# A planned attention and maxout kernel: a new order for its head and first ten groups, key values in pairs of chunks, five relu slots

## The chip, the cores and the metric

The kernel runs on one core of a Trainium2 chip. The time is that of one execution on the device, in microseconds (us), taken as the median of several runs. [...] Matmul results lie in PSUM, which has eight banks of 128 partitions by 512 floats; everything else lies in SBUF.

## What is computed

Agent attention is followed by a maxout feed-forward layer. There are 4 batches of 12544 tokens with 128 channels, 49 agents per batch, and a hidden width of 768.

```python
def sm(a, b):
    s = scale * (a @ b.transpose(0, 2, 1))
    s = s - s.max(-1, keepdims=True)
    e = np.exp(s)
    return e / (e.sum(-1, keepdims=True) + 1e-09)
agent_v = sm(agents, k) @ v          # per batch 49 x 128
x = sm(q, agents) @ agent_v          # per token 128
h = np.maximum(np.maximum(x @ w1, x @ w2), x @ w3)
out = h @ w_out
```

## The kernel before

**The algebra.** The kernel never forms x. For each batch it multiplies `agent_v` with weight differences into one array `G` (49 rows, held in both halves of the partitions): `(w3-w1)`, `(w2-w1)`, and a linear part `w1 @ w_out`. The maximum of three is then w1's part plus a maximum of differences, so a query group needs two matmuls per 128 hidden columns, a relu of the first (op `a`, ACT) and a maximum of the second with it (op `x`, DVE). For one of the six column blocks (`FI` = 4) the differences are nested, and both steps are relus on ACT. The part with w1 goes straight to the output as a linear term (`li`).

**Stage one, per batch b:** the keys and values come in chunks of 9 x 128 tokens. For each chunk g: load (`kl`, `vl`), cast to bf16 (`kc`, `vc`), transpose the keys (`kt`, by PE in batch 0, by DMA later), scores against the agents (`ks`), exponential (`kx`, ACT), values times exponentials (`kv`, nine matmuls), and the addition of this product to a running sum (`va`, DVE). The exponentials are summed by POOL (`ea`, `fo`) in batches 1 to 3, by matmuls with ones (`to`) in batch 0. Then the sum is normalised (`nr`) and the products `gp` and their casts `gv` make `G`. In batch 0 this is the head: nothing of the queries' main work can start before `nr0`. Later batches run beside the queries.

**Stage two:** 49 query groups s of 1024 tokens: load `ql`, cast `qc` (POOL), transpose (`qt` and its copy `qe`, or by DMA, `qd`), scores `sc`, exponential `ex`, sums `su` and their reciprocal `re`; for each block f `u`, `a`, `v`, `x`; the output matmuls `p` into two PSUM banks with `li`, scaling `ov` (DVE), store `st`.

**The order.** `graph` (line 208) lists all operations with their engine, what they follow, and which tile slots they use. The order of all of them, with the slot numbers, is written out by hand of a planner in `ORDER` (line 826): each engine executes its operations in that order and waits with semaphores where an operation needs a result or a slot that is not free yet (`Plan.waits`). SP's loads stand in the same order, so a load that waits for a slot holds up the loads behind it. `SLOTS` (line 46) says how many slots each class has: 8 banks `PS`, 13 load tiles `LD`, 3 relu tiles `AS`, 4 tiles each `EK` for exponentials of keys and `VB` for cast values, 13 tiles `R` for maxima, 10 output tiles `OS`. `SPLIT` says which relus are done in halves (two instructions of 512 columns on two separate banks, "u"). `ROWS` says which output matmuls run as pairs on half the array's rows. `warm` matmuls (`wm`, `wn`) in the head work on nothing.

In batches 1 to 3 a chunk's scores, its value product and, for the last chunk, the total share one PSUM bank `m` from `ks` to `va`:

```python
add(f"kv{r}", PE, em.values(b, g, n, m), mm(n, 49), after=[f"kx{r}", f"vc{r}"], use=[m, f"vb{r}", f"e{r}"])
add(f"va{r}", DVE, em.add_values(b, g, m), (0.13, 0.25), after=[f"kv{r}"] + ([f"va{b}.{g - 1}"] if g else []),
    use=[m, plan.tile("VA", f"va{b}")])
```

Of the kernel before, what the change touches and what calls it, by code (L numbers as in the profile page):

```python
# [9 lines left out]
FP32 = mybir.dt.float32  # L10
BF16 = mybir.dt.bfloat16
# [16 lines left out]
rrfrff rrrffr ffrfff ffrfrr rfffff rrrrrr ffffff ffffrr fffrff rfrrfr fffffr ffrfrf rrfrrr fffffr fffffr frffrf fffrrr rfffff  # L28
# [26 lines left out]
class Plan:  # L55
# [152 lines left out]
def graph(plan, em):  # L208
# [6 lines left out]
    add("agl", ACT, em.load_agents, (0.5, 5.0), dma=True)  # L215
    add("agc", DVE, em.cast_agents, (0.42, 0.52), after=["agl"])
    add("agt", PE, em.turn_agents, (0.2, 0.4), after=["agc", "id"], new=[("PS", "agt")])
    add("prep", DVE, em.place_agents, (0.4, 0.5), after=["agt", "ones"], use=["agt"])
    ch = chunks(0)
    for g, (t0, n) in enumerate(ch):  # L220
# [4 lines left out]
        add(f"kt0.{g}", PE, em.k_turn(g, n), mm(n, 128), after=[f"kc0.{g}", "prep"], new=[("PS", f"kT_ps0.{g}", 3)], use=[f"kb0.{g}"])  # L225
# [3 lines left out]
            new=[("EK", f"e0.{g}")], use=[f"s0.{g}"])  # L229
        add(f"to0.{g}", PE, em.totals(g, n), mm(1, n * 49), after=[f"kx0.{g}"], use=[f"e0.{g}", plan.tile("PS", "acc")])  # L230
        m = n if n == KT else 2
        add(f"vc0.{g}", ACT, em.cast("v", "vb", 0, t0, n, ACT, 0, m), act(m * 128), after=[f"vl0.{g}"], new=[("VB", f"vb0.{g}")],
            use=[f"v0.{g}"])
        if m < n:
            add(f"vd0.{g}", DVE, em.cast("v", "vb", 0, t0, n, DVE, m, n), ((n - m) * 0.067 + 0.08, (n - m) * 0.067 + 0.2),
                after=[f"vl0.{g}"], use=[f"v0.{g}", f"vb0.{g}"])
        add(f"kv0.{g}", PE, em.first_values(g, n), mm(n, 49), after=[f"to0.{g}", f"vc0.{g}"] + ([f"vd0.{g}"] if m < n else []),
            use=[f"vb0.{g}", f"e0.{g}", "acc"])
    for g in range(SPARE):
        add(f"wm.{g}", PE, em.warm(f"warm.{g}"), (0.2225, 0.45), after=["id"], new=[("PS", f"warm.{g}")])  # L240
    for g in range(len(ch)):
        add(f"wn.{g}", PE, em.warm(f"warn.{g}", 2), (0.445, 0.67), after=["id", f"vl0.{g}"], new=[("PS", f"warn.{g}")])
    last = len(ch) - 1
    for w in ("w1", "w3", "w2"):
        add(f"l{w}a", SP, em.w_load(w, 0, DFF // 2), new=[("LD", w)], **dma(196))
        add(f"l{w}b", SP, em.w_load(w, DFF // 2, DFF), use=[w], **dma(196))
    add("lwo", SP, em.w_load("wo", 0, DFF), new=[("LD", "wo")], **dma(393))
    add("d31a", DVE, em.differences(C31, "w3", "w1", ((0, DFF // 2),)), (0.43, 0.55), after=["lw1a", "lw3a"], use=["w1", "w3"])
    add("d31b", DVE, em.differences(C31, "w3", "w1", ((DFF // 2, FI * P), (FI * P + P, DFF))), (0.42, 0.54), after=["lw1b", "lw3b"],
        use=["w1", "w3"])  # L250
    add("d32", DVE, em.differences(C31, "w3", "w2", ((FI * P, FI * P + P),)), (0.21, 0.33), after=["lw2b", "lw3b"], use=["w2", "w3"])
    add("d21a", DVE, em.differences(C21, "w2", "w1", ((0, DFF // 2),)), (0.43, 0.55), after=["lw2a", "lw1a"], use=["w1", "w2"])
    add("d21b", DVE, em.differences(C21, "w2", "w1", ((DFF // 2, DFF),)), (0.43, 0.55), after=["lw2b", "lw1b"], use=["w1", "w2"])
    add("cw1", ACT, em.cast_w1, (0.74, 0.87), after=["lw1a", "lw1b"], use=["w1"])
    add("tw1", PE, em.turn_w1, mm(NF, 128), after=["cw1", "prep"], new=[("PS", "tw1")])
    add("ew1", DVE, em.evacuate_w1, dve_half(DFF), after=["tw1"], use=["tw1"])
    add("cwo", POOL, em.cast_wo, (0.77, 0.85), after=["lwo"], use=["wo"])
    add("rs0", DVE, em.reduce_first, (0.5, 0.6), after=[f"to0.{g}" for g in range(last + 1)], new=[("KR", "kr0")], use=["acc"])
    add("rc0", DVE, em.recip_first, (0.35, 0.4), after=["rs0"], use=["kr0"])
    add("nr0", DVE, em.normalise_first, (0.13, 0.25), after=["rc0"] + [f"kv0.{g}" for g in range(last + 1)], new=[("G", "G0")],  # L260
        use=["kr0", "acc"])
    half = DFF // 2
# [50 lines left out]
    for s in range(NQ):  # L313
# [741 lines left out]
```

## Time and profile before

| | us |
|---|---|
| median of 3 runs | 439.33 (438.46 to 439.44) |
| span of the profiled execution, first to last instruction | 436.6 |
| last value cast of batch 0 on ACT, start | 38.47 |
| first relu of group 0 (ACT), start | 41.90 |
| first maximum of group 0 (DVE), start | 43.02 |
| mean time of a maximum over 1024 columns (DVE) | 1.219 |
| mean time of a relu over 1024 columns (ACT) | 1.033 |

The device time of the profiled execution itself is not listed; its span is 2.7 us below the median. In the profile's rows all operations have the line 388, that of the helper that records them, so rows are told apart by their tiles: `AS` is the first relu's output, `R` the maximum's, `OS` the scaled output, `KB`/`VB` cast keys and values, `EK` the exponentials of the keys, `VA` the running sum of values, `avT` the normalised values of the agents, `wall` the weight differences, `G` the product. "<-" in brackets names what ended the wait ahead of an instruction.

### The profile page before, as it was taken

Reading aid. Unit: us, or ns where it says so; the run is one execution under the profiler, and the core shown is the slowest. Engines: PE = TensorE matmul, PEld = TensorE weight load, DVE = VectorE, ACT = ScalarE, POOL = GpSimd, SP = SyncE. Lnnn points to the kernel's source line nnn. Section 1 sums busy time; section 2 is a strip of 40 time slices with the busy share of each in tenths; the row PEclk is TensorE's granted clock in tenths of the full one; section 3 lists DMA queues with packets and bytes.
Section 4 is the critical chain, followed back from the end, with each engine's and each line's share of the span. In section 5 each row is a group of like instructions: output and inputs, shape, how many; then the busy total and the mean of one; then the engine's idle time right before and its main releaser. Section 6 shows DMA issues by size and latency. Waiting matters only on the chain.

```text
span 436.6 us, 14853 instructions
## 1 busy us (share of the span) xinstructions
PE 411.9 (94%) x6488; PEld 256.9 (59%) x6488; DVE 386.6 (89%) x470; ACT 393.9 (90%) x486; POOL 170.0 (39%) x177
## 2 busy tenths in 40 slices
PE   1788999999999999999999999999999999999994
PEld 1464565666666566656656655656656555655574
DVE  1435999999999999999998999899999999999994
ACT  1278999999999999999999899999999999999993
POOL 3541565556655535165525445342531111000000
PEclk9989999999999999999999999999999999999999
DMA  8999999999999999999999999996999994266313
GB/s 310 411 410 383 311 334 372 289 281 343 269 318 342 279 371 298 266 339 285 294 345 261 407 247 278 276 326 143 276 363 290 284 306 98 74 208 208 119 71 125
DMA packets 98107, 122.37 MB, mean 280 GB/s; under 512 B 71479, under 2 KB 74235, under 8 KB 98043
## 3 DMA queue, kind: packets, MB, share of 16 engines
q1 hardware_dynamic: 97552, 121.07, 95.2%
q8 instruction: 51, 0.84, 0.8%
q10 hardware_dynamic: 491, 0.36, 0.3%
q14 instruction: 13, 0.11, 0.1%
HBM read 78.74 MB, written 25.69 MB: 239 GB/s over the span
## 4 chain that ended last, share of the span: by engine, by line
PE 69%; ACT 16%; DVE 7%; DMA 4%; issue 2%; POOL 1%; SPq 0%; POOLq 0%
PE ps L388 69%; ACT AS L388 9%; DVE R L388 6%; DMA LD<-in_k_dram 4%; ACT R L388 2%; ACT ps L388 2%; POOL KB L388 1%; DVE OS L388 1%; ACT EQ L388 1%; ACT VB L388 1%; ACT G L388 1%; ACT EK L388 1%; ACT OS L388 0%; SPq L388 0%; DVE QT L388 0%
## 5 line engine op out<-in xcount | busy, mean ns | idle before, releaser
L388 DVE TENSOR_TENSOR R<-ps,AS 128x1024 bf16<-128x1024 f32 x245 | 293.5, 1219 | 15.1 <-PE ps L388 10.7
L388 ACT ACTIVATE AS<-ps 128x1024 bf16<-128x1024 f32 (+1 forms) x259 | 245.8, 987 | 10.0 <-PE ps L388 7.2
L388 PE MATMUL ps<-EQ,G 49*128 49x512 bf16 (+1 forms) x1248 | 203.3, 370 | 3.5 <-ACT AS L388 0.7
L388 PE MATMUL ps<-wo_bf,R 64*128 64x128 bf16 (+1 forms) x3368 | 194.0, 218 | 1.1 <-issue 0.8
L388 PEld LDWEIGHTS ps<-wo_bf,R 64*128 64x128 bf16 (+1 forms) x3368 | 139.5, 95 | 59.4 <-issue 31.3
L388 PEld LDWEIGHTS ps<-EQ,G 49*128 49x128 bf16 x1248 | 56.4, 93 | 63.8 <-DVE R L388 18.3
L388 POOL CAST QB<-LD 128x1024 bf16<-128x1024 f32 x49 | 50.5, 1040 | 94.6 <-DMA QT<-QB 49.8
L388 POOL CAST KB<-LD 128x1152 bf16<-128x1152 f32 (+2 forms) x45 | 49.8, 1115 | 52.1 <-DMA LD<-in_k_dram 41.8
L388 DVE TENSOR_TENSOR OS<-ps,RC 128x512 f32<-128x512 f32 x96 | 65.4, 682 | 2.6 <-PE ps L388 2.2
L388 POOL CAST VB<-LD 128x1152 bf16<-128x1152 f32 (+1 forms) x33 | 37.4, 1136 | 40.7 <-DMA LD<-in_v_dram 36.5
L388 ACT ACTIVATE ps<-ps 128x1024 f32<-128x1024 f32 x49 | 49.9, 1018 | 2.8 <-PE ps L388 2.2
L388 ACT ACTIVATE R<-ps 128x1024 bf16<-128x1024 f32 x49 | 50.3, 1027 | 1.9 <-PE ps L388 1.6
L388 ACT ACTIVATE EK<-ps 128x441 bf16<-128x441 f32 (+2 forms) x45 | 23.4, 535 | 18.8 <-PE ps L388 18.4
L388 POOL TENSOR_TENSOR EA<-EA,EK 128x441 f32<-128x441 f32 x27 | 27.6, 1022 | 25.4 <-ACT EK L388 25.1
L388 ACT ACTIVATE EQ<-ps 128x512 bf16<-128x512 f32 x49 | 29.9, 610 | 1.0 <-PE ps L388 0.5
L388 DVE COPY KT<-ps 128x1152 bf16<-128x1152 bf16 (+1 forms) x12 | 8.2, 701 | 14.0 <-PE ps L388 14.0
L388 PE MATMUL ps<-QT,agT 128*64 128x512 bf16 (+1 forms) x104 | 19.9, 388 | 0.2
L388 PE MATMUL ps<-G,EQ 49*128 49x128 bf16 x392 | 19.1, 217 | 0.0
L388 PE MATMUL ps<-EK,VB 128*128 128x49 bf16 x392 | 17.4, 186 | 1.6 <-ACT VB L388 1.6
L388 PEld LDWEIGHTS ps<-EK,VB 128*128 128x128 bf16 x392 | 13.9, 97 | 8.1 <-ACT EK L388 4.2
L388 PE MATMUL ps<-agT,KT 128*128 128x49 bf16 x392 | 17.4, 186 | 0.4 <-DVE KT L388 0.4
L388 PEld LDWEIGHTS ps<-agT,KT 128*128 128x128 bf16 x392 | 14.4, 98 | 4.7 <-issue 2.1
(59 smaller groups left out, 177.6 us busy)
## 6 DMA issues: line engine op xcount, KB each, us to landing
LD<-in_q_dram SPq DMA_DIRECT2D x48, 512.0 KB, 7.7
out_dram<-OS SPq DMA_DIRECT2D x48, 512.0 KB, 6.2
LD<-in_k_dram SPq DMA_DIRECT2D x40, 576.0 KB, 7.6
LD<-in_v_dram SPq DMA_DIRECT2D x40, 576.0 KB, 8.4
LD<-in_k_dram SPq DMA_DIRECT2D x3, 512.0 KB, 5.3
LD<-in_v_dram SPq DMA_DIRECT2D x3, 512.0 KB, 6.7
LD<-in_moe_w_dram SPq DMA_DIRECT2D x6, 192.0 KB, 10.6
KT<-KB SPq DMA_TRANSPOSE x33, 7.3
```

Source lines behind the costliest of these rows:

```text
L388: i = call(*args, **named)
```

## The change

- The operations ahead of the first matmul of group 10 stand in a new order. From there on the order is the old one, apart from operations that no longer exist or were moved across that point (`ov.8.1`, two stores and a few loads), and with other slot numbers.
- Batch 0's keys and values come in 12 chunks of 8 and one of 2 instead of ten of 9 and two of 4. Keys are loaded first, most values behind them, into output tiles (`OS`) that are not in use yet. The casts of the values are spread over ACT, POOL and DVE (`VCAST`). The exponentials lie in `R` tiles. The totals get a PSUM bank of their own.
- Each of w1, w2 and w3 is loaded in three parts (columns 0 to 127, 128 to 383, 384 to 767), and the differences and batch 0's `G` are made in these parts. The cast of w1 moves from ACT to POOL.
- In batches 1 to 3 the value products of two chunks are added up in one PSUM bank of its own, and `va` runs once per pair: 6 times instead of 11 per batch.
- `AS` has five slots instead of three.
- In groups 0 to 9, 12 relus (2 before) and 21 maxima (none before) are done in halves.
- `G`'s linear part is kept in two column blocks, each filled in one half of the partitions only, the rest set to zero once by POOL (`gz`); the matmuls of `li` read their block. (A variant over the whole array, `out_linear_half`, exists and is not used: `LINEAR` is "b" everywhere.)
- The casts `gv` are given to engines by `OUTS`; in batches 1 and 2 one more of them is on DVE.
- `wn` issues three matmuls instead of two, for 13 chunks.

```diff
-FIRST = [KT] * 10 + [4, 4]
+AGAIN = (3,) * 13
+CUTS = {"a": (0, P), "b": (P, 3 * P), "c": (3 * P, DFF)}
+FIRST = [GT] * 12 + [2]
...
 SPLIT = """
-...... u..... .u.... ...... ...... ...... ...... ...... ...... ...... .u.u.. uu.... ...... ...... ...... ...u.. ..u... ......
+v.v..b vbvv.. v.u..v uv.... .....v uv.v.u ..v... .b.u.v v.vb.b .uuv.. .u.u.. uu.... ...... ...... ...... ...u.. ..u... ......
...
+LINEAR = "bbbbbbbbbbbbbbbbbbbbbbbbbbbbbbbbbbbbbbbbbbbbbbbbb"
+VCAST = "aapapapppaaad"
+CASTW = "p"
+OUTS = ("aaadadd", "addda", "addda", "adada")
...
-SLOTS = {"PS": 8, "LD": 13, "QB": 3, "KB": 3, "VB": 4, "KT": 4, "QT": 4, "EQ": 4, "EK": 4, "AS": 3,
+SLOTS = {"PS": 8, "LD": 13, "QB": 3, "KB": 3, "VB": 4, "KT": 4, "QT": 4, "EQ": 4, "EK": 4, "AS": 5,
...
+    add("gz", POOL, em.clear_linear, (0.6, 0.7), after=["id0"])
...
-        add(f"vl0.{g}", SP, em.kv_load("v", 0, t0, n), new=[("LD", f"v0.{g}")], **dma(n * 65.536))
+        add(f"vl0.{g}", SP, em.kv_load("v", 0, t0, n), new=[("OS" if g < 10 else "LD", f"v0.{g}")], **dma(n * 65.536))
...
-            add(f"kv{r}", PE, em.values(b, g, n, m), mm(n, 49), after=[f"kx{r}", f"vc{r}"], use=[m, f"vb{r}", f"e{r}"])
-            add(f"va{r}", DVE, em.add_values(b, g, m), (0.13, 0.25), after=[f"kv{r}"] + ([f"va{b}.{g - 1}"] if g else []),
-                use=[m, plan.tile("VA", f"va{b}")])
+            if g % 2 or g == len(ch) - 1:
+                two = [(x, ch[x][1]) for x in range(g // 2 * 2, g + 1)]
+                y, h = f"{b}.{g // 2}", f"y{b}.{g // 2}"
+                add(f"kv{y}", PE, em.values(b, two, h), mm(sum(x[1] for x in two), 49), after=[f"{z}{b}.{x}" for x, _ in two for z in ("kx", "vc")],
+                    new=[("PS", h)], use=[f"{z}{b}.{x}" for x, _ in two for z in ("vb", "e")])
+                add(f"va{y}", DVE, em.add_values(b, g // 2, h), (0.13, 0.25), after=[f"kv{y}"] + ([f"va{b}.{g // 2 - 1}"] if g > 1 else []),
+                    use=[h, plan.tile("VA", f"va{b}")])
...
+                if SPLIT[s][f] in "vb":
+                    vs = [f"{v}.{h}" for h in range(2)]
+                    add(v, PE, em.hidden(vs, s, f, C21, True), pe, mode=ROW, after=[f"ex.{s}"] + needs(1), new=[("PS", x) for x in vs],
+                        use=[e] + gs)
+                    for h in range(2):
+                        add(f"x.{s}.{f}.{h}", DVE, em.max_second(vs[h], s, f, h), (0.6, 0.72), after=[v, f"{a}.{h if SPLIT[s][f] == 'b' else 0}"],
+                            use=[vs[h], a, r])
...
+    def clear_linear(self):
+        for i in range(SLOTS["G"]):
+            self.nc.gpsimd.memset(self.slots["G", i][:, C1O:], 0.0)
...
     def product_out(self, b, c0, c1, base, name, eng):
         def fn():
             src, out = self.t[name][:, c0 - base:c1 - base], self.t[f"G{b}"][:, c0:c1]
-            if eng == ACT:
-                self.nc.scalar.activation(out, src, AF.Copy)
-            else:
-                self.nc.vector.tensor_copy(out=out, in_=src)
+            cuts = [(src, out)] if c0 < C1O else [(src[h * H:(h + 1) * H, :], self.t[f"G{b}"][h * H:(h + 1) * H, c0 + h * C:c1 + h * C]) for h in range(2)]
+            for src, out in cuts:
+                if eng == ACT:
+                    self.nc.scalar.activation(out, src, AF.Copy)
+                else:
+                    self.nc.vector.tensor_copy(out=out, in_=src)
...
 ORDER = """
...
+vc0.7/0 kv0.7 to0.10 kx0.3/10 vc0.5/2 wn.5/2 to0.3 vl0.4/6 wn.3/2 vc0.0/1 vc0.3/3 wn.0/5 wn.4/2 sc.0/4 kv0.3 vl0.8/7 vc0.8/0 wm.2/1 kv0.8
+to0.8 vl0.6/8 wn.6/1 to0.2 vl0.11/2 to0.0 rs0/0 wn.11/2 vl0.2/9 vc0.4/3 kv0.4 vc0.6/0 kv0.6 kv0.5 wn.8/2 kv0.0 gz rc0 lw2a/5 lw1a/7 d21a
+vc0.11/3 ex.0/0 kv0.11 lw1b lw3b/4 d31b vc0.2/0 kv0.2 nr0/0 gpb0/1 gvb0 lw3a d31a gpa0/4 gva0 gpd0/2 lw2b d21b gpe0/5 u.0.1/0,1 gve0
...
```

More of the change, by code (lines that the diff above doesn't have):

```diff
@@ L228, in graph @@
         add(f"kx0.{g}", ACT, em.k_exps(0, g, n, f"s0.{g}"), (n * 0.041 + 0.07, n * 0.041 + 0.2), after=[f"ks0.{g}"],
[L229 to L232, printed above, removed]
+            new=[("R" if g < 9 else "EK", f"e0.{g}")], use=[f"s0.{g}"])
@@ L233, in graph @@
+        add(f"to0.{g}", PE, em.totals(g, n), mm(1, n * 49), after=[f"kx0.{g}"], use=[f"e0.{g}", plan.tile("PS", "tot")])
+        eng = ENGINES[VCAST[g]]
+        add(f"vc0.{g}", eng, em.cast("v", "vb", 0, t0, n, eng, 0, n), act(n * 128), after=[f"vl0.{g}"], new=[("VB", f"vb0.{g}")],
             use=[f"v0.{g}"])
-        if m < n:
-            add(f"vd0.{g}", DVE, em.cast("v", "vb", 0, t0, n, DVE, m, n), ((n - m) * 0.067 + 0.08, (n - m) * 0.067 + 0.2),
-                after=[f"vl0.{g}"], use=[f"v0.{g}", f"vb0.{g}"])
@@ L247, in graph @@
     add("lwo", SP, em.w_load("wo", 0, DFF), new=[("LD", "wo")], **dma(393))
[L248 to L256, printed above, removed]
+    for x, (c0, c1) in CUTS.items():
+        cuts = ((c0, FI * P), (FI * P + P, c1)) if x == "c" else ((c0, c1),)
+        add(f"d31{x}", DVE, em.differences(C31, "w3", "w1", cuts), dve(c1 - c0), after=[f"lw1{x}", f"lw3{x}"], use=["w1", "w3"])
+        add(f"d21{x}", DVE, em.differences(C21, "w2", "w1", ((c0, c1),)), dve(c1 - c0), after=[f"lw1{x}", f"lw2{x}"], use=["w1", "w2"])
@@ new lines, in graph @@
+                add(f"a.{s}.{f}.0", ACT, em.relu(u, u, None), (0.917, 1.076), after=[u], use=[u])
+                add(v, PE, em.hidden([u], s, f, C21, False), pe, mode=ROW, after=[f"a.{s}.{f}.0"] + needs(1), use=[u, e] + gs)
+                if SPLIT[s][f] == "d":
+                    add(f"x.{s}.{f}.0", DVE, em.relu(r, u, None, DVE), (1.14, 1.28), after=[v], use=[u, r])
+                else:
+                    add(f"x.{s}.{f}.0", ACT, em.relu(r, u, None), (0.917, 1.076), after=[v], use=[u, r])
@@ L352, in graph @@
                 else:
-                    add(u, PE, em.hidden([u], s, f, C31, True), pe, mode=ROW, after=[f"ex.{s}"] + needs("a", "b"), new=[("PS", u, 3)], use=[e] + gs)
-                    add(a, ACT, em.relu(a, u, None), (0.917, 1.076), after=[u], use=[u, a])
-                add(v, PE, em.hidden([v], s, f, C21, True), pe, mode=ROW, after=[f"ex.{s}"] + needs("c", "d"), new=[("PS", v, 3)], use=[e] + gs)
-                add(f"x.{s}.{f}", DVE, em.max_second(v, s, f), (1.14, 1.28), after=[v] + ([f"{a}.{h}" for h in range(2)] if two else [a]),
-                    use=[v, a, r])
@@ L358, in graph @@
-        lin = ["gvl" if p[0] == 0 else f"gvl{p[0]}" for p in parts]
+                    add(u, PE, em.hidden([u], s, f, C31, True), pe, mode=ROW, after=[f"ex.{s}"] + needs(0), new=[("PS", u, 3)], use=[e] + gs)
+                    add(f"{a}.0", ACT, em.relu(a, u, None), (0.917, 1.076), after=[u], use=[u, a])
+                if SPLIT[s][f] in "vb":
[5 more added lines that the diff above has]
+                            use=[vs[h], a, r])
+                else:
+                    add(v, PE, em.hidden([v], s, f, C21, True), pe, mode=ROW, after=[f"ex.{s}"] + needs(1), new=[("PS", v, 3)], use=[e] + gs)
+                    add(f"x.{s}.{f}.0", DVE, em.max_second(v, s, f, None), (1.14, 1.28), after=[v] + [f"{a}.{h}" for h in range(1 + (SPLIT[s][f] == "u"))],
+                        use=[v, a, r])
```

600 lines of the change are left out of this document (317 added, 283 removed).

## The prediction

> **What bounds the kernel now.** I read the page's busy line and tenths first, then the windows, the waits, the groups by shape, and the timeline of the start.
>
> ```profile
> span 436.6 us, 14853 instructions
> PE 411.9 (94%) x6488; PEld 256.9 (59%) x6488; DVE 386.6 (89%) x470; ACT 393.9 (90%) x486; POOL 170.0 (39%) x177
> PE   1788999999999999999999999999999999999994
> DVE  1435999999999999999998999899999999999994
> ACT  1278999999999999999999899999999999999993
> PE 69%; ACT 16%; DVE 7%; DMA 4%; issue 2%; POOL 1%; SPq 0%; POOLq 0%
> ```
>
> A slice is 10.9 us. Three engines are full from the fifth slice to the last but one; only the first four have room. The chain of waits runs over PE for 69% of its length, but with ACT and DVE inside it: there is no single bound. The windows put numbers on both stages (columns: busy us of PE, PEld, DVE, ACT, POOL with counts, clock, DMA share, GB/s; the two rows with four columns show PE alone):
>
> ```profile
> 20.00:25.00 5.00, 4.12 (x60) 1.00 1.02 406
> 25.00:30.00 5.00, 3.81 (x62) 0.70 1.03 412
> 35.00:40.00 5.00, 4.18 (x58) 1.00 1.05 382
> 42.00:60.00 18.00, 16.79 (x254) 9.75 (x254) 17.23 (x22) 17.69 (x26) 10.45 (x10) 1.00 1.07 339
> 60.00:80.00 20.00, 19.85 (x320) 12.22 (x314) 18.93 (x23) 18.81 (x22) 13.62 (x15) 1.00 1.17 303
> 80.00:100.00 20.00, 19.91 (x346) 13.17 (x344) 19.56 (x24) 18.72 (x23) 10.37 (x10) 1.00 1.09 327
> 100.00:122.00 22.00, 22.00 (x332) 13.44 (x328) 21.12 (x28) 20.97 (x26) 15.45 (x16) 1.00 1.10 305
> 122.00:430.00 308.00, 304.56 (x4870) 188.24 (x4869) 294.00 (x341) 295.62 (x361) 105.85 (x110) 1.00 0.93 260
> ```
>
> Until 40 us the DMA engines are full at about 0.41 MB per us: the head is bound by its loads. From 42 us on, groups 0 to 9 take until 122. There DVE is busy 17.23+18.93+19.56+21.12 = 76.8 of 80 us and ACT 76.2: **3.2 and 3.8 us** of idle time is all that a better order of these groups can win. In 122 to 430 DVE idles 14.0 us, ACT 12.4, and PE is full by its modelled ends.
>
> **The change, part by part.**
>
> *The head.* First its end in the trace of before:
>
> ```profile
> 37.99 0.59 ACT L388 ACTIVATE EQ<-ps 128x512 bf16<-128x512 f32 x1
> 38.47 1.16 ACT L388 ACTIVATE VB<-LD 128x1152 bf16<-128x1152 f32 x1
> 39.12 0.56 DVE L388 TENSOR_TENSOR wall<-LD,LD 128x384 bf16<-128x384 f32 x1 [0.70 <-DMA LD<-in_moe_w_dram]
> 40.13 0.21 DVE L388 TENSOR_TENSOR avT<-ps,KR 128x49 bf16<-128x49 f32 x1 [0.45 <-PE ps L388]
> 41.90 3.87 ACT L388 ACTIVATE AS<-ps 128x1024 bf16<-128x1024 f32 x4
> 43.02 1.22 DVE L388 TENSOR_TENSOR R<-ps,AS 128x1024 bf16<-128x1024 f32 x1
> 31.78 1.04 POOL L388 CAST QB<-LD 128x1024 bf16<-128x1024 f32 x1 [1.49 <-DMA LD<-in_q_dram]
> 0.95 0.20 POOL L388 MEMSET ident<- 128x128 bf16 x1 [0.51 <-SPq L822]
> 1.88 5.52 DMA LD<-in_k_dram
> ```
>
> The last value cast ends at 39.63, the normalisation (`nr0`, avT) follows at 40.13, the first relu at 41.90, the first maximum at 43.02. After the change, as before, 13.37 MB of keys, values and first queries are loaded up to the last value tile. At 0.41 MB per us from 1.9 us that is 34.5 us. A cast starts later than this sum: the query cast waited for its load until 31.78, and 11.01 MB make 28.8, a lag of 3.0. So the last values land near 37.5. They are now cast by POOL, not behind two casts and an exponential on ACT: the POOL queue holds three casts of 1.04 us for tiles that by the same sum land from 32.4 to 35.0, then `gz` (four memsets twice as wide as the 0.20 us one, some 1.0 us), then the last cast. That ends near 38.9, and `nr0` comes near 39.5, **0.6 us** earlier. The weight loads in three cuts matter little: the first relu needs columns 128 to 383, whose loads end at 13.76 MB, the same bytes after which the subtraction ran at 39.12. The last cut ends at 14.55 MB in both, near 40.4; the subtractions and a cast behind it put the first maximum near 42.3. I take **-0.7** for the start; ends -1.1 (without `gz` and lag) and 0 (`nr0` still waits for the weights). The longer warm-up matmuls (thirteen times three, not twelve times two) and the thirteenth chunk's instructions lie in 10 to 40 us under the loads, where PE has room (4.12 and 3.81 of 5); were the loads faster, they would cost their own time, at most a few us.
>
> *Added and removed work in groups 0 to 9 and behind.*
>
> ```profile
> L388 DVE TENSOR_TENSOR R<-ps,AS 128x1024 bf16<-128x1024 f32 x245 | 293.5, 1219 | 15.1 <-PE ps L388 10.7 <-ACT AS L388 1.2
> L388 DVE TENSOR_TENSOR OS<-ps,RC 128x512 f32<-128x512 f32 x96 | 65.4, 682 | 2.6 <-PE ps L388 2.2
> 45.23 3.48 DVE L388 TENSOR_TENSOR R<-ps,AS 128x1024 bf16<-128x1024 f32 x3
> L388 ACT ACTIVATE AS<-ps 128x1024 bf16<-128x1024 f32 x231 | 230.9, 1033 | 7.8 <-PE ps L388 5.2
> L388 ACT ACTIVATE AS<-ps 128x512 bf16<-128x512 f32 x28 | 15.4, 604 | 2.2 <-PE ps L388 2.0
> 50.72 1.08 ACT L388 ACTIVATE AS<-ps 128x512 bf16<-128x512 f32 x2 [0.28 <-PE ps L388]
> L388 DVE TENSOR_TENSOR VA<-ps,VA 128x49 f32<-128x49 f32 x30 | 5.9, 197 | 0.3
> L388 DVE CAST G<-ps 128x384 bf16<-128x384 f32 x8 | 4.1, 549 | 0.0
> L388 ACT ACTIVATE G<-ps 128x384 bf16<-128x384 f32 x8 | 4.0, 505 | 0.5 <-PE ps L388 0.5
> L388 ACT ACTIVATE G<-ps 128x128 bf16<-128x128 f32 x4 | 1.2, 304 | 0.0
> ```
>
> Maxima split in halves are new: 21 of them (16 "v", 5 "b"). The nearest row is the 128x512 scaling, 682 ns. By durations a split costs 2 x 0.682 - 1.219 = 0.145; three full ones in a row took 3.48, so starts lie 1.13 apart and 0.09 of each is overlap, which leaves 0.055. Between these ends I take 0.10, for the overlap shows in most rows: **+2.1** (1.2 to 3.0). [...]
>
> Fifteen of 33 additions of key values go: 0.11 to 0.20 each, so -1.6 to -3.0; I take **-2.0**. Two `gv` casts of 384 columns, one each in batches 1 and 2, go from ACT to DVE (+0.9 and -0.85). The linear part of G is written twice, in halves of the partitions: batch 0's moves to DVE (+0.4; ACT -0.3), the other three stay (ACT +0.6). Ten more relus are split: 0.06 each (the pair at 50.72 took 1.08, a full one 1.02) to 0.175 (by durations), I take 0.1 as the row of the pair is nearer: +1.0. Sum: **DVE +1.4, ACT +0.45**. Of that, idle time can hide all or nothing; on engines 96% busy I put **+0.8** on the end (0 to +1.4). The cast of w1 leaves ACT for POOL, which is busy 10.45 of 18 us there.
>
> *Pairs of chunks.* The matmuls of a pair stand at the second chunk's old place, so what is behind them on PE (output matmuls) waits no longer than before; the first chunk's wait is gone. Values get a PSUM bank of their own, and scores give theirs back after the exponential. What they now free shows in the waits:
>
> ```profile
> PEld ps L388 <- DVE R L388: 18.6, 74, 0.6
> PEld ps L388 <- ACT AS L388: 16.0, 61, 0.6
> PEld ps L388 <- ACT EK L388: 4.4, 13, 0.4
> PEld ps L388 <- DVE VA L388: 3.8, 13, 0.4
> ```
>
> Fifteen of 33 additions gone is 3.8 x 15/33 = 1.7 us of PE's waits; a third of the 4.4 may go too. PE carries 69% of the chain: I take 0.69 x 1.7 = **-1.2** (0 to -3.2).
>
> *Five relu slots, kept order.* No row of the waits shows ACT's AS waiting for DVE's R, so the third slot never was short: 0. From group ten the order is the old one. SP's queue is rearranged up to there: in the new order stores 1, 4 and 5 still follow late, and `ql.3` now stands behind `kt1.0`, which waits for the cast `kc1.0`:
>
> ```profile
> 45.15 1.15 POOL L388 CAST KB<-LD 128x1152 bf16<-128x1152 f32 x1 [0.61 <-DMA LD<-in_k_dram]
> 58.63 0.68 DVE L388 COPY QT<-ps 128x1024 bf16<-128x1024 bf16 x1
> LD<-in_q_dram SPq DMA_DIRECT2D x48, 512.0 KB, 7.7
> ```
>
> Issued near 47 and landed 7.7 us later, cast (1.04) and turned, its tile is ready near 56.5 at the latest. DVE took it up at 58.63 (`qe.3`); in the new order it stands behind the first maximum (42.3) and some 14 us of DVE work (eight maxima, six of them split at about 1.24, and half a ninth are 10.3; two query copies, two scalings and the copies between make the rest), so at about 56. It is covered, but thinly: each us by which it comes later stops PE (`qt.3`, with the next group's first matmul behind it) for that us, 0 to +2; I take 0. The new order of groups 0 to 9 itself I put at 0: it can win at most 3.2 us and lose as much.
>
> Sum: -0.7 + 0.8 - 1.2 = **-1.1**. The profiled execution's span of 436.6 becomes 435.5; around the span lie 439.33 - 436.6 = 2.7 us (median of the runs; that execution's own device time isn't listed), which gives **438.2 us**.
>
> **The rivals.**
>
> *Slower: DVE becomes the bound of groups 0 to 9.* Splits at 0.145 (3.0), the moved casts (1.3), less five additions there (1.0) are 3.3 us for an engine that has 3.2 us of idle time in that stretch. It decides if the new order leaves as much idle as the old. Then 439.3 - 0.7 (start) + 3.3 - 1.0 (ten additions later) = **440.9**. For it: DVE at 96% there. Against: ACT and PE also wait there, and split halves let DVE start earlier.
>
> *No difference.* The head's gain and the pairs' gain are taken up by the added work, as all three engines carry more: **439.3**. For it: all terms are near 1 us, with both signs.
>
> *Fuller gain.* Halves and free banks close half of the 3.2 us idle in the first ten groups (-1.6) and the start gains 1.1: 439.3 - 1.6 - 1.1 - 1.2 + 0.4 = **435.8**.
>
> *A cold clock at the start.* In 25 to 30 us the granted clock was 0.70 though PE was busy 3.81 of 5, so 0.30 x 5 = 1.5 us of its clock were withheld. If such a drop fell on 39 to 44 us, the first relus would wait that much longer for PE: 438.2 + 1.5 = **439.7**. [...]
>
> **How the numbers follow.** Forecast 438.2 (own range 437.0 to 438.4): 0.33. Fuller gain: 0.14. No difference 0.21 and cold clock 0.05. Slower: 0.27. About 0.2% (0.9 us) is what a measurement of this kernel tells from no change. Faster 0.47, same 0.26, slower 0.27. The range reaches from the fuller gain with 0.4 more of the waits (435.4) to the slower case without the start's gain and a little more (441.8).
>
> **What would show it.** `nr0` near 39.5, the first maximum near 42.3; PE's waits for VA below 2.5 us; DVE idle in groups 0 to 9 below 3 us for the forecast, above 3 for the slower case; group 10's first relu before 122 us or after. A head that ends at 38 or 41 us, or new waits of POOL, SP or ACT behind EK or VB slots (four each, now held over a pair), would make it wrong.

## The result, and the profile after

The changed kernel is slower, where 438.2 us, a gain, was predicted; it is slower, too, than the slower rival's 440.9.

| | median us | ratio to the kernel before, 95% interval |
|---|---|---|
| before, same chip | 438.89 (438.14 to 439.44, 4 runs) | |
| changed | 444.6 (443.14 to 445.22, 4 runs) | 1.013 (1.0111 to 1.0149) |
| before, second comparison | 438.31 (437.7 to 440.08, 17 runs) | |
| changed, second comparison (after_again) | 442.91 (442.7 to 444.01, 6 runs) | 1.0105 (1.0087 to 1.0122) |

So the loss is 4.6 to 5.7 us. The page and the waits of the changed kernel's first trace (its helper's line is 416 now; in its rows PE runs the matmuls, PEld their weight loads, DVE, ACT and POOL the casts, sums and other work on tensors, and SP issues transfers):

```profile
span 443.3 us, 14837 instructions
PE 416.5 (94%) x6476; PEld 256.7 (58%) x6476; DVE 389.0 (88%) x482; ACT 390.6 (88%) x493; POOL 176.2 (40%) x188
PE 60%; ACT 14%; DMA 10%; DVE 7%; issue 4%; POOL 2%; SPq 2%; POOLq 0%; DVEq 0%
PEld ps L416 <- DVE R L416: 25.9, 79, 4.3
PEld ps L416 <- DMA KT<-KB: 2.9, 4, 1.2
PEld ps L416 <- DVE VA L416: 2.7, 8, 0.5
```

DVE carries 2.4 us more and ACT 3.3 less than before, in a span that is 6.7 us longer: hardly more work, but more gaps. PE's share of the chain of waits fell from 69% to 60%, DMA's rose from 4% to 10%. The wait for `VA` fell from 3.8 to 2.7 us (the prediction had named 2.5), and nothing was won by it. The wait for `R` rose by 7.3; 4.3 of that is one new wait (the longest, last number) in the head, under the loads. The head itself, by the timelines of DVE and ACT:

```profile
39.47 0.21 DVE L416 TENSOR_TENSOR avT<-ps,KR 128x49 bf16<-128x49 f32 x1
42.59 2.41 DVE L416 TENSOR_TENSOR R<-ps,AS 128x1024 bf16<-128x1024 f32 x3
40.95 1.94 ACT L416 ACTIVATE AS<-ps 128x1024 bf16<-128x1024 f32 x2
```

`nr0` at 39.47 and the first maximum at 42.59 stand 0.7 and 0.4 us before the old kernel's 40.13 and 43.02. The windows of the first ten groups, of groups 10 to 26, of 26 to 35, and of the rest, for the changed kernel and then for the old one (columns: PE, PEld, DVE, ACT, POOL busy, clock, DMA share, GB/s):

```profile
42.00:122.00 80.00, 76.60 (x1168) 47.03 (x1167) 75.28 (x109) 74.23 (x99) 43.76 (x42) 1.00 1.11 315
122.00:262.00 140.00, 136.67 (x2154) 84.04 (x2151) 130.89 (x154) 130.97 (x170) 71.12 (x75) 1.00 1.05 304
262.00:345.00 83.00, 81.58 (x1264) 49.22 (x1262) 77.77 (x88) 79.87 (x98) 32.66 (x34) 1.00 1.05 282
345.00:430.00 85.00, 84.09 (x1308) 50.12 (x1308) 82.74 (x90) 82.64 (x94) 7.28 (x7) 1.00 0.53 159
```

```profile
42.00:122.00 80.00, 78.55 (x1234) 48.59 (x1232) 76.84 (x94) 76.19 (x94) 49.89 (x48) 1.00 1.11 317
122.00:262.00 140.00, 139.09 (x2200) 86.72 (x2198) 132.32 (x161) 133.64 (x173) 67.72 (x71) 1.00 1.11 311
262.00:345.00 83.00, 81.95 (x1271) 49.58 (x1272) 79.08 (x94) 81.07 (x98) 31.89 (x33) 1.00 1.07 278
345.00:430.00 85.00, 83.52 (x1408) 51.94 (x1403) 82.59 (x88) 80.91 (x91) 6.24 (x6) 1.00 0.52 159
```

Up to 345 us PE, DVE and ACT have all become idler, in 122 to 345 too, where the order was called the old one. The first row of a second trace of the changed kernel (after_again, below) differs:

```profile
42.00:122.00 80.00, 79.37 (x1209) 48.69 (x1205) 77.61 (x113) 76.87 (x104) 45.48 (x44) 1.00 1.08 327
```

There DVE and ACT are fuller than the old kernel's: the first ten groups differ from one execution to the next, and the loss behind them does not (by the table below 4.46 us from group 10 to 48 in one trace, 4.45 in the other).

**How the place of a loss is read.** Both kernels execute the same first relu in every group, so its start in one trace minus its start in the other is the loss up to there. A step from one group to the next is lost between these two. The starts, in us, for the old kernel's first trace, and the differences from it of the second traces and of the experiments told below:

| first relu of group | 0 | 1 | 10 | 13 | 24 | 36 | 48 |
|---|---|---|---|---|---|---|---|
| before, first trace | 41.90 | 49.21 | 123.10 | 148.83 | 238.53 | 333.50 | 420.93 |
| before_again | -0.12 | -0.01 | -0.01 | -0.01 | 0.00 | 0.00 | 0.00 |
| changed, first trace | -0.95 | 0.00 | 2.32 | 4.32 | 5.09 | 6.78 | 6.78 |
| after_again | 0.15 | 0.42 | 0.28 | 1.71 | 2.48 | 4.72 | 4.73 |
| before_pairs1 | -0.27 | -0.13 | 0.74 | 0.74 | 0.75 | 0.61 | 0.78 |
| before_pairs | -0.93 | -0.81 | -0.04 | -0.10 | 0.63 | 1.52 | 1.52 |
| move_only | -0.23 | -0.11 | 0.33 | 0.27 | 0.73 | 2.43 | 2.43 |
| dbl_odd | 0.53 | 0.52 | 0.72 | 0.71 | 1.60 | 2.34 | 2.34 |
| dbl_even | 0.64 | 0.64 | 0.64 | 0.88 | 1.53 | 1.97 | 1.97 |
| one_even | -0.75 | -0.26 | -0.23 | -0.29 | -0.37 | -0.54 | -0.51 |

The second trace of the changed kernel splits the 4.6 us of its span thus: 0.4 to group 1, nothing in groups 1 to 10 (-0.1), 1.4 in groups 10 to 13, 3.0 in 13 to 36, nothing to group 48, and -0.1 behind it. Batch 3's last pair stands in group 34: the loss ends with the keys and values. In groups 13 to 36 much of it comes in steps of 0.23 us (between the first relus of groups 16 and 17, 21 and 22, 28 and 29, 31 and 32, among others), and 0.23 us is nine value matmuls of 26 ns (the median distance of their starts behind 42 us in both kernels' first traces). A larger step, 0.6 us between groups 24 and 26, is a pause of PE that has nothing to do with the values; such pauses stand in many of the traces below, and the last section tells what the traces show of them.

### The profile page after: what moved, and what is told of

Same layout as the page of the kernel before. It is cut to its first block, busy times and chain, and to the rows that moved or that the text cites. A ratio compares the mean times of both kernels' runs of the same rounds, so it can differ in the third digit from the quotient of the medians.

```text
span 443.3 us, 14837 instructions
## 1 busy us (share of the span) xinstructions
PE 416.5 (94%) x6476; PEld 256.7 (58%) x6476; DVE 389.0 (88%) x482; ACT 390.6 (88%) x493; POOL 176.2 (40%) x188
## 4 chain that ended last, share of the span: by engine, by line
PE 60%; ACT 14%; DMA 10%; DVE 7%; issue 4%; POOL 2%; SPq 2%; POOLq 0%; DVEq 0%
PE ps L416 60%; ACT AS L416 8%; DVE R L416 6%; DMA OS<-in_v_dram 4%; DMA LD<-in_k_dram 3%; DMA KT<-KB 3%; ACT R L416 3%; SPq L416 2%; POOL KB L416 2%; ACT ps L416 1%; ACT EQ L416 1%; POOL VB L416 1%; DVE OS L416 1%; ACT G L416 0%; ACT EK L416 0%
## 5 line engine op out<-in xcount | busy, mean ns | idle before, releaser
L416 DVE TENSOR_TENSOR R<-ps,AS 128x1024 bf16<-128x1024 f32 (+1 forms) x266 | 294.7, 1134 | 16.4 <-PE ps L416 11.9
L416 PEld LDWEIGHTS ps<-EQ,G 49*128 49x128 bf16 x1248 | 55.5, 93 | 67.7 <-DVE R L416 19.9
L416 ACT ACTIVATE R<-ps 128x1024 bf16<-128x1024 f32 (+1 forms) x58 | 54.6, 944 | 19.2 <-PE ps L416 18.9
L416 ACT ACTIVATE EK<-ps 128x441 bf16<-128x441 f32 (+2 forms) x37 | 19.4, 532 | 6.0 <-PE ps L416 5.9
L416 DVE COPY KT<-ps 128x1024 bf16<-128x1024 bf16 (+1 forms) x13 | 8.2, 658 | 11.8 <-PE ps L416 11.7
L416 DVE COPY QT<-ps 128x1024 bf16<-128x1024 bf16 x21 | 14.3, 683 | 2.8 <-PE ps L416 2.8
L416 PEld LDWEIGHTS ps<-G,EQ 49*128 49x128 bf16 x392 | 13.5, 94 | 4.8 <-PE ps L416 0.8
```

Of the source, the lines that this page charges most:

```text
L416: i = call(*args, **named)
```

## The experiments

My first theory after the result was P: the pairs lose in the kept order, since nine matmuls of the first chunk now lie in full on PE's way at the second chunk's place, and win nothing at the place that they left. Rivals: the loss there is drift or other banks and slots (D, B), or PE is simply the bound and matmuls cost the same everywhere (A).

**Pairs undone, pairs alone.** In the changed kernel, batches 2 and 3 one chunk at a time again (and with it the totals of these two batches back in the chunk's bank):

```diff
-            if g % 2 or g == len(ch) - 1:
+            if b in SINGLE:
+                add(f"kv{r}", PE, em.values(b, [(g, n)], m), mm(n, 49), after=[f"kx{r}", f"vc{r}"], use=[m, f"vb{r}", f"e{r}"])
...
+            elif g % 2 or g == len(ch) - 1:
```

> The changed kernel, with the value products of batches 2 and 3 one chunk at a time again, each at the old order's place, in the bank of its chunk's scores. Theory P (pairs): nine matmuls of 26 ns that are moved behind the second chunk cost 0.23 us there in full, and win nothing at the place they leave, since PE has slack there; about eleven such places from group 12 to 36 make the 2.5 us that the changed kernel loses there. Then 444.6 - 2.5 = 442.1 (441.6 to 442.6), and the first relus keep a constant distance from the old kernel's behind group 12. Rival D (drift): the loss behind group 12 comes of other slot numbers and of the state in which group 12 is reached. Then 444.6, within 0.4. Prediction's term (a pair saves PE's wait for the sum): 445.0 or more.

Measured: 442.86 us, ratio 1.0102 (1.0079 to 1.0126). That lies between the changed kernel's two medians, so the times decide nothing. In the trace the difference from the old kernel stays 1.86 to 1.87 from group 13 to 20 (the changed kernel's grew by 0.4 there), but 2.8 us go between groups 24 and 26, where PE pauses for 1.51 us and its clock falls behind the pause (last section). With groups 24 to 26 left out, the traces do decide: from group 13 to 36 the changed kernel loses 2.36 and 2.37 us in its two traces, and the three kernels with these pairs undone (this one, and unpair23_share1 and mend3 below) lose 0.83, 0.78 and 0.80. So the pairs of batches 2 and 3, with their totals' banks, cost 1.6 us in the changed kernel; 0.25 of it stands at batch 3's total.

The reverse, from the old kernel, agrees. In the old kernel, pairs in batches 2 and 3 only:

```diff
-            add(f"kv{r}", PE, em.values(b, g, n, m), mm(n, 49), after=[f"kx{r}", f"vc{r}"], use=[m, f"vb{r}", f"e{r}"])
+            two = [(g, n)] if b == 1 or g == len(ch) - 1 else [(g - 1, ch[g - 1][1]), (g, n)] if g % 2 else []
+            if two:
+                add(f"kv{r}", PE, em.values(b, two, m), mm(sum(x[1] for x in two), 49), after=[f"{z}{b}.{x}" for x, _ in two for z in ("kx", "vc")],
+                    use=[m] + [f"{z}{b}.{x}" for x, _ in two for z in ("vb", "e")])
```

> The old kernel, with only the value products of batches 2 and 3 in pairs, at the second chunk's place, in the second chunk's bank; order and banks otherwise as they were. Theory P: +0.23 us for each of eight pairs, 1.8 us or a little more, so 440.5 to 441.4 where the old kernel has 438.9. Prediction's term: 0.4 us less per batch at the most, 438.1 to 438.9. Rival D: no difference, within 0.4 of 438.9.

Measured: 440.38, ratio 1.0053 (1.0034 to 1.0072): +2.1 us by the medians, +2.3 (1.5 to 3.2) by the ratio. In the trace 1.56 come from group 10 on, where these pairs stand; another 0.77 in group 6 is a pause of PE, ahead of all of them. The same with batch 1 alone:

> The old kernel with pairs in batch 1 alone (chunks 0 to 9, groups 1 to 10), at the second chunk's place and in its bank. By the run with pairs in batches 2 and 3 (+2.1 for two batches): +1.0 (0.5 to 1.6), 439.5. If the first ten groups have room for it: within 0.4 of the old kernel's 438.5. What the changed kernel loses beyond the pairs of three batches is then the new order's: 444.6 less the old kernel's time with all pairs.

Measured: 439.28, ratio 1.0018 (1.0006 to 1.0029), +0.8 us; in the trace 0.87 from group 1 to 10. Pairs alone, put into the old kernel, cost 2.4 us by the traces and some 3 by the medians, of the 4.6 to 5.7. The prediction's term was -1.2.

**Why: matmuls added, taken away, moved.** Three edits of the old kernel leave order, banks, slots and waits alone and change only how many value matmuls a chunk of batches 2 and 3 issues. Doubled at chunks 1, 3, 5, 7, 9:

```diff
-        return lambda: self.product_values(self.t[m][:, CV:CV + A], self.t[f"vb{b}.{g}"], self.t[f"e{b}.{g}"], n)
+        def fn():
+            if b > 1 and g % 2 == TWICE and g < 10:
+                self.product_values(self.t[m][:, :A], self.t[f"vb{b}.{g}"], self.t[f"e{b}.{g}"], n)
+            self.product_values(self.t[m][:, CV:CV + A], self.t[f"vb{b}.{g}"], self.t[f"e{b}.{g}"], n)
+        return fn
```

> The old kernel, with the nine value matmuls of chunks 1, 3, 5, 7 and 9 of batches 2 and 3 issued twice (the second product goes to columns of the bank that nobody reads afterwards); nothing is left out, moved or put in another bank. These are the places at which the pairs have 18 matmuls. Theory P (PE is short of time at these places, each burst of nine matmuls costs 9 x 25.8 ns = 0.23 us in full): 0.23 at seven to ten places, +1.6 to +2.3 us over the old kernel's 438.3, and steps of 0.23 in the first relus behind group 12. Rival B (the pairs lose by banks and slots that are held longer, not by matmuls): no difference, within 0.4.

> The same with chunks 0, 2, 4, 6 and 8: the places that the pairs leave. Theory P (PE has slack there, so that nothing is won by leaving them): no difference, within 0.5 of the old kernel. Rival A (every matmul of PE costs its time wherever it stands): +2.3 us, as at the other places; then the pairs should have won at one place what they lose at the other.

Measured: 439.46, ratio 1.0018 (1.0005 to 1.003), and 439.52, ratio 1.0014 (1.0005 to 1.0023). Both cost about 0.7 us; my "no difference" for the even places missed. In the traces the steps are the 0.23 us, 1.6 and 1.3 us in groups 10 to 36. Then eight of nine matmuls taken away at the even chunks (`1 if few else n` for the count):

> The old kernel with one value matmul instead of nine for chunks 0, 2, 4, 6 and 8 of batches 2 and 3: 80 matmuls of 25.8 ns are left out, 2.1 us of PE, at the places that the pairs leave. Theory C (three balanced engines: what PE gets more it is late by, what it gets less it waits for ACT and DVE): less than 0.5 us faster than the old kernel's 438.5. Rival A (PE alone is the bound there): 1.3 to 2.1 us faster, as the doubled products cost steps of 0.23 us in the trace; then pairs must lose by something else than their place.

Measured: 437.23, ratio 0.9973 (0.9958 to 0.9988), 0.5 to 1.8 us faster, which is rival A's side. But from group 1 to 48 the trace shows 0.25 us. Of the rest, 0.26 lies ahead of group 1, and 0.97 near the end, where PE pauses in the old kernel inside a run of eight matmuls (first two rows; "issue" means that the profile shows nothing that PE waited for) and in one_even does not (third row):

```profile
427.81 0.23 PE L388 MATMUL ps<-wo_bf,R 64*128 64x128 bf16 x1
428.83 0.38 PE L388 MATMUL ps<-wo_bf,R 64*128 64x128 bf16 x7 [0.79 <-issue]
```

```profile
427.30 0.40 PE L388 MATMUL ps<-wo_bf,R 64*128 64x128 bf16 x8
```

Both doubled kernels lack this pause too, and all three come 0.97 us earlier from it on; every trace of the old kernel and of its variants with the same number of matmuls has it (0.63 to 0.92). So their medians are 0.97 too low as prices of the value matmuls: +1.7 and +1.6 to 1.8 for the doubled ones, -0.2 for the one with fewer, near the traces' +1.8, +1.3 and -0.25 from group 1 to 48. Added matmuls cost most of their 2.3 us at either place, and those taken away win next to nothing, which is not rival A. This was read off one trace each. A further run moved the matmuls and nothing else:

```diff
+            some = b > 1 and g < 10
+            if some and g % 2:
+                self.product_values(self.t[m][:, :A], self.t[f"vb{b}.{g}"], self.t[f"e{b}.{g}"], n - 1)
+            self.product_values(self.t[m][:, CV:CV + A], self.t[f"vb{b}.{g}"], self.t[f"e{b}.{g}"], 1 if some and g % 2 == 0 else n)
```

> The old kernel in which only the value matmuls of batches 2 and 3 change places: chunks 0, 2, 4, 6 and 8 issue one of their nine products, chunks 1, 3, 5, 7 and 9 their nine and eight more, into columns that nobody reads. PE has the same number of matmuls; banks, slots, waits and DVE's additions are the old kernel's. The sums of the even chunks lack eight of nine products. Theory P (what a place gets more costs 0.23, what a place loses wins little): +1.3 to +2.1 us over the old kernel, as the pairs in these batches do (+2.1). Rival B (the pairs lose by banks, slots and waits; matmuls cost and win the same): -0.5 to +0.3, the sum of the two runs that added at one place (+0.7) and took away at the other (-1.3).

Measured: 440.1, ratio 1.004 (1.0025 to 1.0055), +1.75 us (1.1 to 2.4). That settles it between P and B: the move alone costs most of what the pairs cost, without their banks and slots. (Of the 2.5 us of its trace from group 1 on, 0.4 lie ahead of group 10 and of all that was moved, 0.97 between groups 30 and 32 are a pause of PE, and 1.1 are the steps, where the pairs have 1.56.) PE's timeline shows how. At an even chunk's place, old kernel, then move_only:

```profile
171.71 0.40 PE L388 MATMUL ps<-EK,VB 128*128 128x49 bf16 x9
172.07 0.77 PE L388 MATMUL ps<-EQ,G 49*128 49x512 bf16 x4
```

```profile
172.11 0.19 PE L388 MATMUL ps<-EK,VB 128*128 128x49 bf16 x1
172.47 0.77 PE L388 MATMUL ps<-EQ,G 49*128 49x512 bf16 x4 [0.17 <-DVE R L388]
```

move_only comes here 0.40 late and leaves 0.40 late, with eight matmuls fewer: what is next on PE waits for a bank that DVE frees, and the old order had put the nine matmuls into that gap, where they cost nothing. So it is at two of the ten even places; at the other eight the next work on PE starts 0.15 to 0.21 us earlier, and at seven of them that is lost again within 0.2 to 2.1 us (at two of them by a wait for ACT, 0.17 and 0.27 us). At the next odd chunk's place, old kernel, then move_only:

```profile
179.69 0.39 PE L388 MATMUL ps<-EK,VB 128*128 128x49 bf16 x9
180.02 0.82 PE L388 MATMUL ps<-EQ,G 49*128 49x512 bf16 x6
```

```profile
180.10 0.60 PE L388 MATMUL ps<-EK,VB 128*128 128x49 bf16 x17
180.63 0.82 PE L388 MATMUL ps<-EQ,G 49*128 49x512 bf16 x6
```

Here nothing is waited for: it comes 0.41 late and leaves 0.61 late. The 0.20 us are the eight matmuls, and they stay: the table's steps. At nine of the ten odd places the trace shows 0.21 to 0.22 of this kind.

**The price of halves.** In the old kernel, the 21 maxima of groups 0 to 9 by two instructions each:

```diff
+            for at in [(slice(None), h) for h in range(2)] if s < 10 and HALVES[s][f] == "v" else [slice(None)]:
+                self.nc.vector.tensor_tensor(out=r[at], in0=v_[at], in1=a[at], op=ALU.max)
```

> The old kernel with the 21 maxima of groups 0 to 9 that the changed kernel has in halves done by two instructions of 512 columns each, one behind the other; order, banks and waits are as they were. The price of the split alone: by the prediction's 0.10 each on a full DVE +2.1 over the old kernel's 438.5 (1.2 to 3.0 by its two bounds); if the 3.2 us of idle time that DVE has in groups 0 to 9 hide it, within 0.5.

Measured: 438.66, ratio 1.0002 (0.9988 to 1.0016): +0.1 us (-0.5 to 0.7). In its trace the first relus lose 0.4 us from group 1 to 10. Its page and the row of its halves:

```profile
PE 410.8 (94%) x6488; PEld 255.9 (59%) x6488; DVE 388.0 (89%) x491; ACT 394.2 (90%) x486; POOL 170.0 (39%) x177
L389 DVE TENSOR_TENSOR R<-ps,AS 128x512 bf16<-128x512 f32 x42 | 26.9, 682 | 1.4 <-PE ps L389 1.2
```

DVE is busy 388.0 us against 386.6: 1.4 for 21 splits, 0.07 each. The second half starts 0.60 us after the first, 0.08 before the first one's row ends; a split maximum takes 1.28 us where the same one whole took 1.22. The reverse, whole maxima in the changed kernel:

> The changed kernel with the 21 maxima of groups 0 to 9 whole instead of in halves; relus and order as they are. If the halves cost what the prediction took (0.10 each) and DVE is the bound there: 444.6 - 2.1 = 442.5. If they cost 0.145: 441.6. If they cost nothing since DVE has 6.5 us of idle time in groups 0 to 10: 444.6. If the order was made for them and whole maxima start later: above 445.

Measured: 463.34, ratio 1.0567 (1.0541 to 1.0592). Not a price of halves: a whole maximum frees both its banks later, and tiles of two banks had to be put elsewhere. PE's own waits for `R` became 17.7 us (5.8 in the changed kernel), and its granted clock, 1.00 in the changed kernel from 42 us to the last groups, was 0.52 in 51.5 to 55 us, 0.50 in 58.5 to 68.5 and 0.51 in 133.5 to 137. It shows only that the new order, in these banks, needs its halves.

**The new head with the old order.** Three trials, each with the changed kernel's head and the old order behind it, joined ahead of group 0, group 1 and group 2:

> The changed kernel's head up to its first relu, five relu slots, weights in three cuts, the linear part in blocks; behind it the old order of groups 0 to 9, with the old halves and the old rows, values one chunk at a time in all batches, and the casts of G on the old engines. If the head's gain lasts (a.0.1 stands 1.0 us earlier in the changed kernel) and all the loss lies in the new order of groups 0 to 9, their halves and the pairs: 437.9 (437.4 to 438.4). If the head's gain is lost in group 0 to 2 whatever the order, because the key and query loads set the pace there: 438.9. If five slots, the linear blocks or the moved bank numbers cost time: above 439.5.

> The changed kernel's head and its order of group 0 up to the first matmul of group 1, five relu slots, weights in three cuts, the linear part in blocks; from group 1 on the old order with the old halves, rows, banks and engines of the casts, values one chunk at a time. If the first trial of this kind lost its 2.9 us by the order that I had given group 0 there (between the first relus of groups 0 and 1): 438.3 less the head's gain, so 437.3 to 438.3. If what lies behind the head costs time whatever the order (five slots, linear blocks, the load order at group 0): 440 to 443.

> The same, with 17 more maxima of groups 1 to 9 in halves, those that the changed kernel has in halves there, in the old order and in the old banks: 21 in all. The prediction's price of 0.10 each on a full DVE: +1.7 over the kernel without them; by the upper price, 0.145: +2.5. If DVE's idle time in groups 1 to 9 hides it, or the earlier start of a half pays for it: within 0.4.

> A third trial of the new head with the old order, now with the changed kernel's order as far as the first matmul of group 2 (halves of groups 0 and 1 with it), and the old order, halves, rows, banks and casts from there; values one chunk at a time everywhere; five relu slots, linear blocks. If the loss sits in the order of groups 2 to 9 and in the pairs: 437.6 to 439.2. If the order of groups 0 and 1, or what the late loads of queries 3 and 4 do behind it, is the loss: 440 to 443.

Measured: 443.17 (ratio 1.0102, 1.0079 to 1.0126), 443.91 (1.0123, 1.0104 to 1.0143), 444.92 with halves (1.0141, 1.0124 to 1.0159), and 447.02 (1.0198, 1.0169 to 1.0227). They tell little of the head: by their traces each loses 3 to 7 us within three groups of its joint, in an order that is my own there and neither kernel's, and 0.6 to 1.3 us from group 4 to 48. Part of the loss at the joint is the clock, which falls to 0.51 in 49 to 56 us (headold2), 0.50 in 48 to 54.5 (headold2_v) and 0.52 in 64 to 67.5 (headold3). So five relu slots, the linear blocks and the moved slots together cost the old order no more than 0.6 to 1.3 us there; whether the new head would serve it stays open. 0.15 to 0.19 and 0.3 of it come between groups 23 and 24 and groups 35 and 36, just where `G` of batches 2 and 3 is made with its linear part written twice, and the changed kernel loses 0.15 and 0.31 there in both traces; no run has the blocks alone, so this is argued from the place. The halves in headold2_v, 1.0 us, are within the two intervals.

**Groups 3 and 10 to 13.** In the first trace of the changed kernel PE waits in group 3 for the transposed keys; the same place in its second trace:

```profile
65.82 0.61 PE L416 MATMUL ps<-ident,QB 128*128 128x128 bf16 x8
67.46 0.40 PE L416 MATMUL ps<-agT,KT 128*128 128x49 bf16 x9 [1.03 <-DMA KT<-KB]
```

```profile
65.41 0.61 PE L416 MATMUL ps<-ident,QB 128*128 128x128 bf16 x8
65.86 0.39 PE L416 MATMUL ps<-agT,KT 128*128 128x49 bf16 x9
```

> The changed kernel as it is, for a second trace. If its wait for the transposed keys of chunk 2 (1.03 us of PE at 67.5) comes in every execution, it stands in this trace too, and group 3's first relu starts 1.8 us later against the old kernel's than group 2's; if it comes by the landing of loads, it is shorter or missing here. 444.6 in either case, 443 to 445.3 by execution.

> The old kernel as it is, for a second trace. How far one execution differs from another with the same code: the start of the first relu (41.9 in the first trace; the kernels with the same head gave 41.0 to 42.6) and the length from the last group's first relu to the end (15.7). If both scatter by 0.5 or more, a gain of 0.7 in the head can't be read from one pair of traces.

Measured: 442.91 (1.0087 to 1.0122) and 438.36, one run. The wait depends on when the transposed keys land: group 3 starts 1.8 us later than group 2 did, against the old kernel, in one execution and 0.6 in the other, and 0.6 of either is made up by group 4. It is part of what the first trace loses more than the second. The new order asks for these scores ahead of group 3's first relu (`kx1.2` at 67.89, relu at 68.33); the old one asked behind it. Moving them did not help:

> The same, and the scores of chunk 2 of batch 1 and their exponential stand later in group 3 (behind the second hidden matmuls of block 1, and the relu of block 3), so that the keys' transposition has about 3 us more. In the changed kernel's trace PE waits 1.03 us there, ACT 1.37, DVE 1.18. If that wait comes in most executions: 0.7 to 1.5 us less than without this edit, 440.0 to 441.0. If it comes in few (in another trace of this order it did not show): no difference, within 0.4.

Measured: 443.58, ratio 1.0114 (1.0088 to 1.0139): no difference from the run without this edit (443.55, below).

```profile
71.24 0.39 PE L423 MATMUL ps<-EQ,G 49*128 49x512 bf16 x2 [1.50 <-ACT EK L423]
```

PE now waits 1.50 us for the exponential to give its bank back: the wait has only moved. The other place, in the second trace of the changed kernel:

```profile
130.97 0.42 PE L416 MATMUL ps<-ES,ones 128*128 128x49 f32 x2 [0.18 <-DVE R L416]
131.64 0.47 DVE L416 RECIPROCAL KR<-ps 128x49 f32<-128x49 f32 x1 [0.72 <-PE ps L416]
131.97 1.02 ACT L416 ACTIVATE R<-ps 128x1024 bf16<-128x1024 f32 x1 [0.55 <-PE ps L416]
```

Batch 1's total has a bank of its own now and waits for DVE to free it; DVE and ACT then wait for PE. With the total in the value products' bank:

> The changed kernel with the value products of batches 2 and 3 one chunk at a time, as in the run of that kind (442.86), and batch 1's total in the bank of its last value product, as scores, products and total shared one in the old kernel, instead of in a bank of its own. In the changed kernel's trace this total waits at 133 us for DVE to free its bank, and DVE, ACT and PE then idle 0.7, 0.6 and 0.3 us. If that wait is the loss between groups 10 and 13 (1.9 us): 441.0 to 441.8. If the loss there comes of the 18 matmuls of the pair in front of the total: 442.9, no difference.

Measured: 443.55 (441.24 to 445.77), ratio 1.0108 (1.0078 to 1.0138): the times scatter too widely to tell. By the trace the loss in groups 10 to 13 is 0.73 us, and 0.73 in mend3, which shares the bank too; it is 1.48 in unpair23, 1.43 in after_again and 2.00 in the first trace, where the bank is its own. So the bank is 0.7 of it.

## Why the prediction was wrong, step by step

- **Pairs of chunks, -1.2.** This step failed, and with it the sign. "The matmuls of a pair stand at the second chunk's old place, so what is behind them on PE waits no longer than before": what is behind them comes 0.23 us later at most pairs, nine matmuls at a place without a gap. And "the first chunk's wait is gone" is true and worth nearly nothing: PE waits for another bank there, or a little later. Alone, the pairs cost +0.8 and +2.3 us. I had priced the waits and not the matmuls that were moved; multiplying a sum of waits by PE's share of the chain has no ground where the next wait ends 0.17 us later.
- **Kept order, "the old one".** Failed for the same reason: it lost 3.0 us in groups 13 to 36. 1.6 of them go with the pairs and their totals' banks, 0.6 are a pause of PE, 0.8 stay when the pairs are undone.
- **Added work, +0.8.** The halves were taken too high, but inside the stated bounds: 2.1 us of DVE predicted, 1.4 measured, 0.07 each, and in the time 0.1 (-0.5 to 0.7), by the trace 0.4. (By the rows, two halves of 0.682 less a whole one of 1.219 make 0.145; the second half starts 0.08 us before the first one's row ends, which leaves 0.07.) The mechanism of the slower rival, DVE as the bound of groups 0 to 9, finds no support either, though its side came true: DVE idles 2.4 us there in the second trace and 4.7 in the first, and the halves alone cost the old kernel little.
- **New order of groups 0 to 9, 0.** Right in the second trace (-0.1 from group 1 to 10, with five pairs inside that cost the old order 0.9), +2.3 in the first. The sign "group 10's first relu before 122 us" was of no use: the old kernel's own starts at 123.10.
- **The head, -0.7.** `nr0` and the first maximum came nearly as predicted in the first trace, and by the way predicted (POOL's last cast of values ends at 39.00, 38.9 was said); in the second they came at 39.97 and 43.36. The old head's first relu came anywhere from 40.97 to 42.55 in nine traces of the same head, the new one's from 40.87 to 42.05 in five. Neither confirmed nor refuted; and by group 1 the changed kernel had nothing left of it in either trace (0.00 and +0.42).
- **Not foreseen:** the total's own bank, 0.7 of the 1.4 us in groups 10 to 13 for batch 1, 0.25 more for batch 3; and the pause of PE between groups 24 and 26. The prediction looked at the slots that pairs hold, not at the order in which a new bank comes free.
- **Five relu slots, 0, and the cold clock:** five slots were not run alone. The granted clock of the changed kernel is 1.00 at 40 to 45 us in its first trace and 1.00 at 42 to 122 in its second, so the cold-clock rival's condition did not come about; where the clock did fall in an experiment, the last section tells.
- **What lies around the span, 2.7:** an execution of the old kernel lasts 1.8 us longer than its span (436.6 and 438.36 in before_again). By that the profiled execution was the fastest of the three, 0.9 below their median; this moves the forecast's 438.2 and not its change of -1.1.

Of the 4.6 us of the second comparison, by the traces: 0.4 stand ahead of group 1; 1.4 in groups 10 to 13, 0.7 of them the total's bank; and 3.0 behind, of which the pairs and the later totals make 1.6, the pause 0.6, and 0.8 stay without the pairs. Batch 1's pairs cost 0.9 in the old order, and what made up for them in the new order of groups 1 to 10 is not settled, nor are the other 0.7 of groups 10 to 13. Nothing that I ran beats the old kernel with its full computation.

## What to carry to other kernels

In a planned order on balanced engines, small work has been put into gaps, and costs nothing there: before merging or moving it, look at what its neighbours wait for at the old place and at the new one, and price the work itself, not only the wait that goes. Matmuls that were added cost 1.3 to 1.8 of their 2.3 us here; those that were taken away won 0.25 of 2.1, down to the next engine's wait. To see it, align the two traces operation by operation and look for steps. And before a difference of under 1 us between two programs is read as the price of an edit, look for pauses without a releaser: here one of 0.63 to 0.92 us was missing in the three variants of the old kernel whose number of matmuls an edit had changed.

## What the runs showed of the hardware

Two executions of the old kernel agree within 0.01 us in the first relu of every group shown from group 1 to group 48, 372 us, although their starts differ by 0.12. Starts that differ by more persist: 0.5 us in dbl_odd up to group 7. So in these traces the scatter is made at the start, in single waits for transfers and in pauses of PE.

A maximum over 1024 columns takes 1.219 us, its halves 0.682 each, and the split costs DVE 0.07 us of busy time: between the prediction's bounds of 0.055 and 0.145, near the lower.

**Pauses of PE without a releaser.** In after_again PE pauses for 0.91 us at 253.4, and the profile names no releaser ("issue"):

```profile
254.26 0.39 PE L416 MATMUL ps<-EQ,G 49*128 49x512 bf16 x2 [0.91 <-issue]
```

At the same matmul the changed kernel's first trace has 0.36, and unpair23 1.51 two matmuls ahead of it; the old kernel's has 0.25 just ahead of there. The page lists a queue that brings instructions; in the old kernel:

```profile
q8 instruction: 51, 0.84, 0.8%
```

These are 51 packets of 16 KiB, 0.84 MB in all. PE's records (matmuls, weight loads and the sequencer's) number 13107, 257 for each packet. All traces together have 22 pauses of PE over 0.3 us behind 42 us without a releaser. Behind each of them PE goes on with a record whose number, counted from 0 and divided by 256, leaves 193 to 195, and does so 1.30 to 1.59 us after such a packet has landed. I read this as PE having used up one block of instructions before the next was there. The doubled kernels have 52 packets and one_even has 50: counted so, the blocks end at other matmuls there, and the pauses at the end are missing. That the blocks are the cause is read from these places and times; no run was made to test it, and what makes a block come late I did not follow up.

**The clock behind a pause.** In unpair23 the granted clock falls 1.7 us after the pause of 1.51 us, for 3.4 us in which PE is busy nearly all the time:

```profile
256.00:258.00 2.00, 1.83 (x23) 1.15 (x23) 1.15 (x2) 1.64 (x3) 0.00 (x0) 0.53 0.12 27
258.00:260.00 2.00, 2.00 (x26) 1.29 (x23) 1.16 (x3) 0.98 (x2) 1.22 (x2) 0.62 0.00 0
```

This makes the other 1.3 of the 2.8 us that this trace loses between groups 24 and 26. Behind after_again's pause of 0.91 us the clock stays at 1.00.
